# A transform chunk loaded one chunk later, and the two heads' maxima begun level

## The chip, the cores and the metric

The kernel runs on one core of a Trainium2 chip. The metric is device time in microseconds (us) of one execution; the time of the kernel before is the median of three timed executions, and its profile comes from one further execution. In the profile PE is the matrix engine's matmuls and PEld its weight loads, DVE the vector engine, ACT the scalar engine, POOL the GpSimd engine, and SP the queue from which nearly all transfers are issued.

## The reference

```python
def reference(A_x, A_dft_seq_re, A_dft_seq_im, A_dft_hid_re, A_dft_hid_im, B_x, B_wqkv, B_wo, gate_w):
    x = A_x                                    # 1 x 2048 x 512
    g = sigmoid((x * gate_w).sum(-1, keepdims=True))
    a = x @ A_dft_hid_re.T ; b = x @ A_dft_hid_im.T
    y = A_dft_seq_re @ a - A_dft_seq_im @ b    # 2048 x 2048 by 2048 x 512
    q, k, v = heads(x @ B_wqkv)                # 32 heads of 16
    p = softmax(q @ k.T * 16 ** -0.5)          # per head 2048 x 2048
    o = merge(p @ v) @ B_wo
    return g * y + (1 - g) * o
```

Everything is float32. The large products are made in three passes from a rounded part and a rest ("hi" and "lo"), which the kernel calls `h1, l1` or `ch, cl`.

## The kernel before

**Two streams beside each other.** The 32 heads are 16 pairs. Head 0 of a pair lies in the upper half of the partitions, head 1 in the lower half, from partition 64 on. A matmul on one half of the rows of PE runs beside one on the other half. So the kernel puts the transform (the DFT, matmuls with output `d` at L416) on one half and one head's attention on the other, and swaps the halves from segment to segment.

**The attention of a pair** has three kinds of work on PE. Maxima (`a_tile`, L222): a tile of raw scores, of which DVE takes the row maxima (L224). Scores (L722): the same product with the maxima folded in as two further rows, of which ACT makes exponentials (L723). Values (L758): the exponentials times v. The maxima of a head run `LEAD = 48` tiles ahead of its scores, out of 64 tiles for each head of a pair. The stacks `qs` and `ks` hold q and k of one pair; there are two of each, so pair p uses those of pair p-2. `load_stacks(p)` fills both with twelve transfers, six for head 0 first and then six for head 1 (L209, L210). It is put in line at unit 32(p-1)-1 of the plan, just ahead of the values of the last units of pair p-2, and its transfers wait until the last scores of that pair have read the stacks.

**The order is written out.** A segment is one half: a pattern of slots (`FULL`, for the 96 pairs of segments that carry the transform), each slot a transform matmul and beside it a score or a maximum of the other head, and at `|` the values. Even segments serve head 1, odd ones head 0. `FULL` has 16 slots with eight scores and eight maxima; the maxima are in slots 1, 4, 5, 8, 9, 11, 13 and 14, counted from 0.

**The start.** `four(range(4), *wre, ...)` makes the last rows ahead of the segments in four phases of twelve paired matmuls (L315). After matmuls 3 and 8 of a phase it calls `first_tiles`, which in the kernel before does something after matmul 3 only: a score of head 0 and a maximum of head 1, side by side.

**The transform's matrix** comes in 128 chunks of 256 KB (`w_seq`). `c_load` (L361) puts a chunk into one of two staging tiles (`craw`, in turn), `c_split` (L371 and L372, on POOL) makes `ch` and `cl` from it, which have three places in turn. Both are called from `dft_next` at the end of chunk i: `c_split(i + 3)` and then `c_load(i + 5)`, whose staging tile is the one that this split reads. A chunk is twelve transform matmuls on each half; of the sixteen that a pair of segments carries, its ends fall at slots 12, 8, and 4 and 16 of three pairs in turn. All transfers from SP are issued in program order and use eight completion semaphores in turn, so that a transfer also waits for the one eight places before it.

**POOL** also adds up the values' partial sums (L773), adds the two halves of the transform (L474) and makes the attention's output parts (`nh`, L85); several SP transfers (`yg`, `oh`, `o`) wait for these.

## Time and profile before

| | us |
|---|---|
| median of three timed executions (lowest, highest) | 1738.22 (1738.08, 1739.89) |
| the profiled execution's own time | 1735.85 |
| its span, first to last instruction | 1733.7 |
| PE busy (share of the span) | 1689.3 (97%) |
| DVE, ACT, POOL busy | 1373.9, 1249.5, 746.5 |
| granted clock of PE, mean | 0.99 |

PE is busy when at least one matmul is under way on it, on either half of its rows. The profile's views used below are the page's summary and chain of waits, the list of waits by engine, tables of busy time by stretch of time, and the timeline, in which rows of equal instructions that follow each other are merged (start, duration, count). In a timeline row the brackets give the idle time of the engine just before it and what ended it; where several semaphores are waited for, or where transfers share one, that name is only the likeliest.

### The profile page before, as it was taken

To read this page: it belongs to the slowest core of one execution; us is meant where nothing else is said; L and a number is where in the kernel's file an instruction comes from. 1 tells how busy PE (TensorE), PEld (TensorE's weight loads), DVE (VectorE), ACT (ScalarE), POOL (GpSimd) and SP (SyncE) were. 2 spreads that over 40 slices of the span, in tenths; PEclk is the share of its full clock that TensorE was granted. 3 is DMA by queue.
4 is the path that set the end of the run, shared out by engine and by line. 5 is a ranking of instruction groups with operands and counts; after the bars stand their busy time and mean duration, and the time that the engine had idled before them with its cause. 6 is when DMAs were issued, how large, how long until landed. Compare 5 with 4: busy or idle time off the path is not lost.

```text
span 1733.7 us, 34488 instructions
## 1 busy us (share of the span) xinstructions
PE 1689.3 (97%) x13072; PEld 1093.2 (63%) x13072; DVE 1373.9 (79%) x2283; ACT 1249.5 (72%) x2472; POOL 746.5 (43%) x807
## 2 busy tenths in 40 slices
PE   9999999999999999999999998999999899999998
PEld 7888766666656665665666665666666566655543
DVE  5448688888878887887888886888888787899954
ACT  5211388877778787777787786777778687787796
POOL 1115544544434555444444564445545456322230
PEclk9999999999999999999999999999999999999999
DMA  9963502113141425123164535133141525631014
GB/s 300 335 143 121 154 8 38 37 50 68 44 74 57 94 87 117 38 65 59 44 176 144 117 110 106 44 68 69 56 86 51 107 86 129 236 61 34 16 42 136
DMA packets 82486, 165.16 MB, mean 95 GB/s; under 512 B 19776, under 2 KB 20032, under 8 KB 78480
## 3 DMA queue, kind: packets, MB, share of 16 engines
q1 hardware_dynamic: 77968, 162.56, 36.1%
q8 instruction: 103, 1.69, 0.4%
q0 software_dynamic: 4352, 0.39, 0.3%
q14 instruction: 63, 0.52, 0.1%
HBM read 107.73 MB, written 54.52 MB: 94 GB/s over the span
## 4 chain that ended last, share of the span: by engine, by line
PE 89%; DMA 7%; SPq 1%; POOL 1%; ACT 1%; issue 1%; DVE 0%; DVEq 0%; POOLq 0%; ACTq 0%
PE d L416 34%; PE t L758 25%; PE t L222 10%; PE t L722 8%; PE t L315 4%; DMA ks<-qk 4%; DMA qs<-qk 2%; PE t L88 2%; PE t L89 2%; PE t L90 2%; PE t L333 1%; DMA craw<-w_seq 1%; PE t L739 1%; SPq L209 1%; SPq L210 1%
## 5 line engine op out<-in xcount | busy, mean ns | idle before, releaser
L224 DVE TENSOR_REDUCE mx<-t 128x1 f32<-128x512 f32 x2022 | 1255.1, 683 | 241.9 <-PE t L222 182.7
L723 ACT ACTIVATE pt<-t 128x512 f32<-128x512 f32 x2048 | 1038.1, 633 | 47.8 <-PE d L416 30.6
L722 PE MATMUL t<-qs,ks 50*128 50x512 f32 x2048 | 743.6, 414 | 0.9 <-ACT y L432 0.9
L222 PE MATMUL t<-ks,qs 48*128 48x512 f32 x2022 | 696.3, 403 | 32.0 <-DMA ks<-qk 17.7
L416 PE MATMUL d<-xab,ch 64*128 64x512 f32 x2016 | 649.3, 397 | 0.0
L758 PE MATMUL t<-pt,vt 128*32 128x512 f32 x3968 | 481.1, 602 | 0.0
L416 PEld LDWEIGHTS d<-xab,ch 64*128 64x128 f32 x2016 | 368.3, 185 | 132.7 <-issue 88.0
L222 PEld LDWEIGHTS t<-ks,qs 48*128 48x128 f32 x2022 | 368.3, 186 | 99.6 <-issue 29.9
L416 PE MATMUL d<-xab,cl 64*128 64x512 f32 x1008 | 400.3, 397 | 0.0
L722 PEld LDWEIGHTS t<-qs,ks 50*128 50x128 f32 x2048 | 368.8, 185 | 34.3 <-ACT pt L723 13.2
L773 POOL TENSOR_TENSOR osum<-osum,oe 128x512 f32<-128x512 f32 x217 | 279.6, 1288 | 169.5 <-ACT oe L767 154.2
L767 ACT COPY oe<-t 128x512 f32<-128x512 f32 x217 | 127.6, 588 | 242.8 <-PE t L758 241.7
L758 PEld LDWEIGHTS t<-pt,vt 128*32 128x32 f32 x3968 | 105.4, 109 | 232.7 <-issue 153.2
L371 POOL CAST ch<-craw 128x512 fp32r<-128x512 f32 x126 | 77.1, 612 | 373.0 <-PE t L722 341.8
L416 PEld LDWEIGHTS d<-xab,cl 64*128 64x128 f32 x1008 | 186.5, 185 | 67.6 <-issue 50.3
L372 POOL TENSOR_TENSOR cl<-craw,ch 128x512 fp32r<-128x512 f32 x126 | 162.1, 1287 | 10.2
L245 POOL DMA_DIRECT2D qs<-mt x128 | 72.0, 568 | 93.0 <-DVE mt L241 86.3
L416 PE MATMUL d<-wo_hl,o_hl 64*128 64x512 f32 (+1 forms) x270 | 72.5, 392 | 0.8 <-DVE yp_qs L597 0.8
L416 PE MATMUL d<-wre,xab 64*128 64x512 f32 x288 | 70.4, 389 | 0.0
L416 PEld LDWEIGHTS d<-wre,xab 64*128 64x128 f32 x288 | 52.9, 185 | 3.9
L416 PEld LDWEIGHTS d<-wo_hl,o_hl 64*128 64x128 f32 (+1 forms) x270 | 49.5, 185 | 4.8 <-DVE yp_qs L597 1.3
L88 PE MATMUL t<-xab,wh 128*128 128x512 f32 x128 | 50.2, 392 | 0.0
(121 smaller groups left out, 891.6 us busy)
## 6 DMA issues: line engine op xcount, KB each, us to landing
craw<-w_seq SPq DMA_DIRECT2D x128, 256.0 KB
qk<-hl SPq DMA_DIRECT2D x32, 512.0 KB
qs<-qk SPq DMA_DIRECT2D x96, 128.0 KB
ks<-qk SPq DMA_DIRECT2D x96, 128.0 KB
b<-hl SPq DMA_DIRECT2D x16, 512.0 KB
xab<-b SPq DMA_DIRECT2D x16, 512.0 KB
o<-osum SPq DMA_DIRECT2D x62, 128.0 KB
oh<-nh SPq DMA_DIRECT2D x12, 512.0 KB
```

Of the source, the lines that this page charges most:

```text
L88: nc.tensor.matmul(ps, sh, mh, start=first, stop=False)
L222: nc.tensor.matmul(ps, qs[p % 2][r, qt * P:(qt + 1) * P], ks[p % 2][r, kb * 512:(kb + 1) * 512], start=True, stop=True)
L224: user = nc.vector.tensor_reduce(mx[p % 2][:, h, qt, kb:kb + 1], ps, AX.X, ALU.max)
L245: (nc.sync, nc.gpsimd)[h].dma_start(rows.rearrange("v (q b c) -> v b q c", q=8, b=4)[:, b], mt[hf][32 * b + h:32 * b + 32:2])
L371: nc.gpsimd.tensor_copy(h1, raw)
L372: nc.gpsimd.tensor_tensor(l1, raw, h1.bitcast(F32), ALU.subtract)
L416: i = nc.tensor.matmul(self.ps, st[r], mv[r], start=not self.begun, stop=stop)
L722: nc.tensor.matmul(ps, ks[p % 2][rr, kt * P:(kt + 1) * P], qs[p % 2][rr, q0:q0 + 512], start=True, stop=True)
L723: return nc.scalar.activation(pts[u][:, 2 * qb + h], ps, AF.Exp, bias=0.0, scale=DH ** -0.5)
L758: nc.tensor.matmul(acc[32 * j:32 * j + 32], vt[:, kt, p, h:h + 32], pt[:, j], start=u == us[0], stop=u == us[-1])
L767: nc.scalar.copy(oe, acc)
L773: nc.gpsimd.tensor_tensor(o, o, oe, ALU.add)
```

## The change

There are two edits. First, `dft_next` calls `c_load(i + 4)` in place of `c_load(i + 5)`, and the extra first load, `c_load(4)`, goes. Chunk i+4 goes into the staging tile that was read by `c_split(i + 2)`, put in line one chunk end before; it is split at the next chunk end. Second, `first_tiles` issues a score of head 0 after matmul 3 and a maximum of head 0 after matmul 8, each alone in its slot, where it issued a score of head 0 and a maximum of head 1 together after matmul 3. After the four phases head 0 has four scores and four maxima done beyond the common lead, and head 1 none; before, head 0 had four more scores and head 1 four more maxima.

```diff
@@ real_next
             c_load(3)
             c_split(2)
-            c_load(4)
@@ dft_next
             c_split(i + 3)
-            c_load(i + 5)
+            c_load(i + 4)
@@ first_tiles
         if j == 3:
-            user = scores(*next(streams[0][0]), turn_of("a"))
-            a_tile(*next(streams[1][1]))
-            return user
+            return scores(*next(streams[0][0]), turn_of("a"))
+        a_tile(*next(streams[0][1]))
```

Lines after `first_tiles` and `real_next` move up by one or two: L722 becomes L721, L758 L757, L776 L775.

On PE, in the first of the four phases of the start (L315 are the phase's own matmuls, `x2` the two halves), before (-) and now (+):

```order
 L315 MATMUL t<-wre_1425,xab_175 128x512 x2
 L315 MATMUL t<-wre_1426,xab_175 128x512 x2
-L722 MATMUL t<-qs_934,ks_936 128x512
-L222 MATMUL t<-ks_936,qs_934 128x512
+L721 MATMUL t<-qs_934,ks_936 128x512
 L315 MATMUL t<-wre_1430,xab_175 128x512 x2
 L315 MATMUL t<-wre_1426,xab_175 128x512 x2
```

```order
 L315 MATMUL t<-wre_1431,xab_175 128x512 x2
 L315 MATMUL t<-wre_1427,xab_175 128x512 x2
+L222 MATMUL t<-ks_936,qs_934 128x512
 L315 MATMUL t<-wre_1428,xab_175 128x512 x2
 L315 MATMUL t<-wre_1432,xab_175 128x512 x2
```

The maximum no longer stands right behind the score, which ran on the other half of the rows; it comes five matmuls later and is of the same half.

On PE, where the first maximum of pair 3 stands (`ks_937` and `qs_935` are pair 3's stacks, `_936` and `_934` pair 2's; the brackets name the semaphores waited for, `DMAHW` those of SP's transfers). Before, an even segment, head 1:

```order
L722 MATMUL t<-qs_934,ks_936 128x512 [waits Activation_49]
L416 MATMUL d<-xab_178,ch 128x512
L222 MATMUL t<-ks_936,qs_934 128x512 [waits DVE_49]
L416 MATMUL d<-xab_178,cl 128x512
L222 MATMUL t<-ks_937,qs_935 128x512 [waits DMAHW5_49,DMAHW4_49,DMAHW6_49,DMAHW1_49,DMAHW7_49,DMAHW0_49,Activation_49]
L416 MATMUL d<-xab_178,ch 128x512
```

Now, the odd segment after it, head 0, and then the first maximum of head 1:

```order
L222 MATMUL t<-ks_936,qs_934 128x512 [waits DVE_49]
L416 MATMUL d<-xab_178,cl 128x512
L222 MATMUL t<-ks_937,qs_935 128x512 [waits DMAHW5_49,DMAHW2_49,DMAHW6_49,DMAHW1_49,DMAHW7_49,DMAHW0_49,Activation_49]
L416 MATMUL d<-xab_178,ch 128x512
...
L757 MATMUL t<-pt,vt 32x512 x7
L416 MATMUL d<-xab_175,ch 128x512 [waits Activation_49,Pool_49]
L721 MATMUL t<-qs_934,ks_936 128x512 [waits DVE_49]
L416 MATMUL d<-xab_175,ch 128x512
L222 MATMUL t<-ks_937,qs_935 128x512 [waits DMAHW5_49,DMAHW6_49,DMAHW4_49,DMAHW7_49,DMAHW3_49,DMAHW0_49]
```

The first use of a new pair's stacks moves by one whole segment, from slot 9 of an even one to slot 9 of the odd one after it; it is head 0's and waits for six transfers, and head 1's first, with six semaphores of its own, follows in slot 1 of the next segment.

On SP, where the transform begins (`craw` are the chunks' loads, `o` the values' sums). Before:

```order
L361 DMA craw<-w_seq 128x512 [waits DMAHW7_49,PE_49]
L361 DMA craw<-w_seq 128x512 [waits DMAHW0_49,PE_49]
L361 DMA craw<-w_seq 128x512 [waits DMAHW7_49,DMAHW1_49,Pool_49]
L776 DMA o_104<-osum 64x512 [waits DMAHW2_49,Pool_49]
L776 DMA o_104<-osum 64x512 [waits DMAHW3_49]
L361 DMA craw<-w_seq 128x512 [waits DMAHW4_49,DMAHW0_49,Pool_49]
```

Now:

```order
L361 DMA craw<-w_seq 128x512 [waits DMAHW7_49,PE_49]
L361 DMA craw<-w_seq 128x512 [waits DMAHW0_49,PE_49]
L775 DMA o_104<-osum 64x512 [waits DMAHW1_49,Pool_49]
L775 DMA o_104<-osum 64x512 [waits DMAHW2_49]
L361 DMA craw<-w_seq 128x512 [waits DMAHW7_49,DMAHW3_49]
L361 DMA craw<-w_seq 128x512 [waits DMAHW4_49,DMAHW0_49,Pool_49]
```

One load is gone from the head of the line, and every later place in it that loaded chunk i+5 loads chunk i+4. The number of the split that such a place waits for on POOL falls by one, so that it names a split of one chunk end earlier; the other transfers keep their order.

## The prediction

> **What bounds the kernel now.** I read the page first, for the engine that ends last.

> ```profile
> span 1733.7 us, 34488 instructions
> PE 1689.3 (97%) x13072; PEld 1093.2 (63%) x13072; DVE 1373.9 (79%) x2283; ACT 1249.5 (72%) x2472; POOL 746.5 (43%) x807
> PE 89%; DMA 7%; SPq 1%; POOL 1%; ACT 1%; issue 1%; DVE 0%; DVEq 0%; POOLq 0%; ACTq 0%
> ```

> PE is the bound, and the change takes no matmul from it. What can be had is PE's idle time, and the chain says of what kind that is: 7% of it are transfers. The list of PE's waits names them:

> ```profile
> PE t L222 <- DMA ks<-qk: 17.7, 3, 8.2
> PE t L222 <- DMA craw<-w_seq: 11.4, 4, 3.9
> PE t L222 <- DMA qs<-qk: 1.5, 1, 1.5
> ```

> Always it is a maximum (L222) that waits. I don't trust the name `craw` there, since no maximum reads a chunk; transfers share eight semaphores, and these waits lie at the same place as the others, a pair's first maximum. So PE stands still where the stacks of the next pair haven't landed.

> How much that costs I take from tables by stretch, the first two rows with the values' matmuls alone (16 to a segment), the third with all engines:

> ```profile
> 597.20:678.70 81.50, 26.94 (x224) 5.87 (x224) 1.00 0.30 92
> 345.10:1497.40 1152.30, 369.10 (x3040) 79.80 (x3040) 0.99 0.35 85
> 345.10:1497.40 1152.30, 1120.34 (x9121) 715.93 (x9120) 956.12 (x1574) 885.73 (x1754) 560.36 (x601) 0.99 0.35 85
> ```

> In an undisturbed stretch 224 / 16 = 14 segments take 81.5 us, 5.82 each. The transform's whole stretch has 3040 / 16 = 190 segments, which would take 1105.8 us at that pace and take 1152.3: **46.5 us too many**, over twelve loads of stacks. PE is idle for 1152.3 - 1120.3 = 32.0 of these. The other 14.5 are a slower PE, which shows behind the stalls (the column ahead of the last two is the granted clock):

> ```profile
> 1073.26 0.39 PE L416 MATMUL d<-xab,ch 64*128 64x512 f32 x1
> 1081.84 0.76 PE L222 MATMUL t<-ks,qs 48*128 48x512 f32 x1 [8.19 <-DMA ks<-qk]
> 1081.90:1085.60 3.70, 3.70 (x17) 2.41 (x21) 2.63 (x4) 1.59 (x3) 0.00 (x0) 0.50 0.24 88
> 790.82 0.47 PE L222 MATMUL t<-ks,qs 48*128 48x512 f32 x1 [2.88 <-DMA craw<-w_seq]
> 792.10:795.40 3.30, 3.30 (x17) 0.87 (x17) 1.71 (x3) 1.19 (x3) 0.00 (x0) 0.50 0.03 5
> 403.51 0.47 PE L222 MATMUL t<-ks,qs 48*128 48x512 f32 x1 [1.48 <-DMA qs<-qk]
> 403.50:405.00 1.50, 1.49 (x13) 1.39 (x13) 0.99 (x2) 0.76 (x2) 0.00 (x0) 1.00 0.02 8
> ```

> After 8.19 us idle, and after 2.88, PE gets half its clock for some microseconds; after 1.48 us, which is pair 3's stall, it keeps it. So a stall of 3 us costs nearly twice itself, and one below 1.5 only itself.

> [...]

> **Why the stacks are late.** The tenth pair's load is the worst. PE's row is the last score that reads the old stacks (slot 6 of its segment); the others are SP's line:

> ```profile
> 1055.13 0.39 PE L722 MATMUL t<-qs,ks 50*128 50x512 f32 x1
> 1046.63 10.35 SPq L361 DMA_DIRECT2D craw<-w_seq  x2
> 1060.27 0.33 SPq L475 DMA_DIRECT2D yg<-y  x1
> 1062.20 0.33 SPq L361 DMA_DIRECT2D craw<-w_seq  x1
> 1064.69 0.59 SPq L558 DMA_DIRECT2D oh<-nh  x1
> 1065.37 0.55 SPq L209 DMA_DIRECT2D qs<-qk  x1
> ...
> 1069.57 0.42 SPq L209 DMA_DIRECT2D qs<-qk  x1
> ...
> 1072.97 0.30 SPq L210 DMA_DIRECT2D ks<-qk  x1
> ...
> 1075.23 1.40 SPq L776 DMA_DIRECT2D o<-osum  x2
> ```

> The stacks are free at 1055.5, the first transfer leaves at 1065.4, 9.9 us later. From there the load needs 16.5 us until PE goes on at 1081.84; its last four pieces are held for the first four to land, 1.1 us apart ((1072.97 - 1069.57) / 3). The segment in question lasted 10 us too long. Pair 3 has the mild form:

> ```profile
> 383.51 0.39 PE L722 MATMUL t<-qs,ks 50*128 50x512 f32 x1
> 386.86 0.33 SPq L361 DMA_DIRECT2D craw<-w_seq  x1
> 387.28 0.38 SPq L209 DMA_DIRECT2D qs<-qk  x1
> ```

> Free at 383.9, left at 387.3: 3.4 us late, and a stall of 1.5. In both a chunk's load stands directly or nearly in front, waiting for the split of the chunk that has just ended, and the list of SP's waits has that as its largest entry:

> ```profile
> SPq L361 <- POOL cl L372: 489.8, 97, 13.0
> ```

> **The change part by part.**

> *The later first use.* The old first maximum of a pair was head 1's fifth of an even segment, the new one is head 0's fifth of the odd segment after it. That is one segment, 5.82 us more. Moreover head 0 needs only the six transfers that go first. In pair 10 they have landed by about 1075.2: the place in line at 1075.23 is eight behind the sixth, and waits for it. They are needed at 1073.65 (the old stall's start) + 5.82 = 1079.5, so 4.3 us are to spare even if the load starts no earlier. Head 1's first then stands in slot 1 of the next even segment: two segments less eight slots later than now, 11.64 - 8 x 0.23 = 9.8 us, so at 1083.4 against a landing by 1081.84: 1.6 us to spare. In pair 3, with a stall of 1.5, both spare more. I see none of the twelve that keeps a stall of its own.

> *The moved load.* At the place ahead of the stacks SP now waits for a split one chunk end earlier, which is long done. In pair 3 the next thing that holds it is the stacks themselves, so the load leaves up to 3.4 us earlier. In pair 10 `oh` still waits for POOL until 1064.69 and little is gained. This is a second cover on top of the first; I count nothing for it. The number of transfers falls by none (128 chunks, each still loaded once), only the line's first place goes.

> So the term is the whole 46.5 us, idle and half clock together, less what is left over: stalls below 1.5 us in one or two pairs, I put 0.5.

> *What the later chunk costs.* A chunk must now land between its place in line and the next chunk end. POOL's split shows the ends, and that until now it waited for PE and never for a transfer:

> ```profile
> L371 POOL CAST ch<-craw 128x512 fp32r<-128x512 f32 x126 | 77.1, 612 | 373.0 <-PE t L722 341.8 <-PE d L416 31.2
> 867.86 0.61 POOL L371 CAST ch<-craw 128x512 fp32r<-128x512 f32 x1 [5.55 <-PE t L722]
> 878.57 0.61 POOL L371 CAST ch<-craw 128x512 fp32r<-128x512 f32 x1 [4.64 <-PE d L416]
> 881.33 0.61 POOL L371 CAST ch<-craw 128x512 fp32r<-128x512 f32 x1 [0.78 <-PE d L416]
> 892.32 0.61 POOL L371 CAST ch<-craw 128x512 fp32r<-128x512 f32 x1 [6.79 <-PE t L722]
> qs<-mt POOLq DMA_DIRECT2D x128, 2.0 KB, 1.7
> ```

> The ends lie 10.7, 2.8 and 11.0 us apart; one in four is close, 32 in all. SP runs ahead, so a chunk usually leaves soon after the split before last, but where something stands in front it may leave at the end itself. How long 256 KB take to land no clean row tells. Below: 1.7 us, what 2 KB take. Above: 4.2 us, from the first piece of pair 10 (1065.37) to the ninth that waited for it (1069.57), plus 1.1 for the second 128 KB, 5.3 us. I take 4, near the upper row, as both are transfers from DRAM of the same order. Then POOL stands up to 1.2 us at a close end, 2.5 at worst. Behind a stack load, which holds the rings for 16.5 us, it may stand some 5. What is queued behind it on POOL: the sums (L773), for which ACT's next-but-one copy waits, and the stores on SP. But the chunk itself is used only three ends after the one where it is put in line, two after its split, over 13 us; and POOL has work for 560.36 of 1152.3 us. I cost it at nothing, with this cover; a hold beyond about 6 us, a segment, would reach ACT through the two buffers of sums.

> *The start.* Four maxima that ran beside a score now stand alone.

> ```profile
> 197.96 2.90 PE L315 MATMUL t<-wre,xab 64*128 64x512 f32 x24
> 200.70 0.39 PE L722 MATMUL t<-qs,ks 50*128 50x512 f32 x1
> 200.71 0.39 PE L222 MATMUL t<-ks,qs 48*128 48x512 f32 x1
> ```

> Twelve paired matmuls take 200.70 - 197.96 = 2.74 us, 0.23 a slot. At least four slots are added, 0.9 us; at most each maximum costs its full 0.39, 1.6 us. I take 1.0, nearest to the row of slots. The last of them frees the transform's bank some five slots later than before, with no room to spare, so nothing is gained here.

> *The sum.* 1735.85 (the profiled execution) - 46.5 + 0.5 + 1.0 = 1690.9 us. The median of the timed runs stands 2.4 us above the profiled one; I carry that over: **1693 us**.

> **The rivals.**

> *The stalls shrink but stay.* Head 0's margin is worked out with loads as they are now. If POOL, held by chunks, gives `oh` and `yg` later, three or four loads leave still later, and each stall of 3 us costs about 5 with its half clock. At most four such: +20, 1713; likelier two of 2 to 3 us, about 1700. For it: pair 10 has only 1.6 us for head 1. Against: the other loads spare more, and SP's largest wait goes.

> *It doesn't do what it says.* If the late start were the transfers' own pace and the added segment were eaten by chunks that now leave ahead of the stacks, each 256 KB (2.2 us at 1.1 per 128 KB), two of them would take 4.4 of the 5.82 us. Each load then gains 1.4 us, with the half clock that goes with it (46.5 / 32.0) 2.0, the twelve 25, and some 22 us stay: 1715. Against it: the chunks are moved, not added.

> *The chunk becomes the wait* (the other side). Mechanism: SP reaches a chunk only at the chunk end, POOL stands at each of the 32 close ends, and PE at the `ch` behind it. Price at the upper bound 2.5 us each, 80 us in all; at that price it would be 1693 + 80 = 1773, slower by 2%. It decides from the point where a chunk's split comes over 13 us late, or POOL holds the sums for more than a segment every time. For it: POOL is in order. Against: both covers are several times the price, and POOL is idle for half of the stretch.

> [...]

> **How the numbers follow.** All stalls gone, 1688 to 1697: 0.74. Stalls shrunk, 1697 to 1713: 0.16. It doesn't do what it says, 1703 to 1737: 0.05, with a fifth of that within 0.2%. The chunk becomes the wait: 0.05, of which 0.02 give back about all and 0.03 end slower. The lower end is the sum without left-overs and without the 2.4 us, should that be stall too: about 1689. Upwards the range goes into the second case until 2 in 10 are left out: 1688 to 1703. A measurement here can tell about 0.2%, 3.5 us, from no change. Faster by more: 0.94; within: 0.03; slower: 0.03.

> **What would show it.** The 190 segments of the stretch at 5.82 us each; no L222 with more than 1.5 us of idle time ahead of it; a granted clock of 1.00 through the stretch; SP's wait at L361 for `cl` far below 489.8 us; the first piece of pair 3's stacks right behind the last score. Wrong would be: a chunk's cast on POOL that waits for `craw` for over 6 us, copies on ACT that wait for POOL's sums, or PE's L416 waiting for `cl`. If the stalls are gone and the time isn't, the half clock or the close ends have taken it.

## The result, and the profile after

| | before | after |
|---|---|---|
| timed median, side by side (us) | 1739.06 | 1689.63 |
| lowest and highest | 1738.08, 1740.63 | 1689.11, 1690.03 |
| profiled execution (us) | 1735.85 | 1689.90 |

The changed kernel takes 0.9715 of the time of the one before (95% interval 0.9698 to 0.9732), 49.4 us less. It was measured twice more beside the experiments: 1690.09 us, 0.9735 (0.9713 to 0.9757), and 1690.52 us, 0.9733 (0.9717 to 0.975).

First the page of the changed kernel, its span, busy times and the chain that ended last:

```profile
span 1688.1 us, 34488 instructions
PE 1676.5 (99%) x13072; PEld 1089.9 (65%) x13072; DVE 1371.2 (81%) x2283; ACT 1246.1 (74%) x2472; POOL 747.3 (44%) x807
PE 98%; POOL 1%; issue 0%; DVE 0%; DMA 0%; ACT 0%; DVEq 0%; POOLq 0%; ACTq 0%
```

The 7% of transfers are gone from the chain. PE's busy time fell too, from 1689.3 to 1676.5 us with as many instructions (13072). These 12.8 us are mainly matmuls that ran at half the clock: by the trace's clock records PE was busy for 20.9 us at 0.50 in the transform's stretch before, and half of that is 10.5. PE's waits, the whole list (engine, line, what was waited for: us in total, times, longest):

```profile
PE t L159 <- DVE wch L156: 2.2, 1, 2.2
PE d L416 <- DVE yp_qs L596: 0.8, 1, 0.8
PE t L666 <- DVE on L660: 0.7, 1, 0.7
PE t L721 <- ACT y L432: 0.5, 1, 0.5
```

No maximum (L222) waits any more. The table by stretch, over the 190 segments of the transform, the values' matmuls alone and then all engines:

```profile
346.00:1452.00 1106.00, 365.55 (x3040) 79.34 (x3040) 1.00 0.37 88
346.00:1452.00 1106.00, 1106.00 (x9121) 711.23 (x9120) 952.93 (x1575) 882.74 (x1754) 560.90 (x601) 1.00 0.37 88
```

The same 3040 matmuls in 1106.0 us in place of 1152.3, PE busy for every one of them, at the full clock. Measured from the first values' matmul of a segment to that of the next, the stretch went from 1152.35 to 1105.87 us, 46.5 less, and each segment lasts 5.82 us, but for one that has 0.26 more in both kernels. Last, what SP waits for:

```profile
SPq L245 <- DVE mt L241: 329.9, 27, 25.4
SPq L775 <- POOL osum L772: 165.5, 17, 18.3
SPq L474 <- POOL y L473: 112.0, 14, 13.9
SPq L470 <- ACT y L469: 97.2, 15, 12.6
...
SPq L361 <- POOL cl L372: 47.3, 26, 5.7
```

The wait for a chunk's split fell from 489.8 to 47.3 us. But the first four grew, from 246.9, 95.6, 36.6 and 18.5: SP waits for what stands next in its line. How much of the gain hangs on this wait at all is what the experiments ask first.

### The profile page after: what moved, and what is told of

Same layout as the page of the kernel before. It is cut to its first block, busy times and chain, and to the rows that moved or that the text cites. A ratio compares the mean times of both kernels' runs of the same rounds, so it can differ in the third digit from the quotient of the medians.

```text
span 1688.1 us, 34488 instructions
## 1 busy us (share of the span) xinstructions
PE 1676.5 (99%) x13072; PEld 1089.9 (65%) x13072; DVE 1371.2 (81%) x2283; ACT 1246.1 (74%) x2472; POOL 747.3 (44%) x807
## 3 DMA queue, kind: packets, MB, share of 16 engines
q8 instruction: 103, 1.69, 0.4%
## 4 chain that ended last, share of the span: by engine, by line
PE 98%; POOL 1%; issue 0%; DVE 0%; DMA 0%; ACT 0%; DVEq 0%; POOLq 0%; ACTq 0%
PE d L416 40%; PE t L757 27%; PE t L222 10%; PE t L721 9%; PE t L315 4%; PE t L89 2%; PE t L88 2%; PE t L90 2%; PE t L333 1%; PE t L738 1%; PE t L416 0%; PE t L159 0%; POOL hl L292 0%; PE t L675 0%; DMA b<-hl 0%
## 5 line engine op out<-in xcount | busy, mean ns | idle before, releaser
L722 ACT ACTIVATE pt<-t 128x512 f32<-128x512 f32 x2048 | 1034.6, 631 | 9.5 <-PE t L721 9.3
L721 PE MATMUL t<-qs,ks 50*128 50x512 f32 x2048 | 740.2, 413 | 0.5 <-ACT y L432 0.5
L222 PE MATMUL t<-ks,qs 48*128 48x512 f32 x2022 | 689.8, 400 | 0.0
L416 PE MATMUL d<-xab,ch 64*128 64x512 f32 x2016 | 644.8, 394 | 0.0
L757 PE MATMUL t<-pt,vt 128*32 128x512 f32 x3968 | 477.5, 598 | 0.0
L416 PEld LDWEIGHTS d<-xab,ch 64*128 64x128 f32 x2016 | 366.7, 184 | 133.3 <-issue 92.2
L222 PEld LDWEIGHTS t<-ks,qs 48*128 48x128 f32 x2022 | 366.5, 186 | 62.4 <-DVE mx L224 27.4
L416 PE MATMUL d<-xab,cl 64*128 64x512 f32 x1008 | 397.9, 395 | 0.0
L721 PEld LDWEIGHTS t<-qs,ks 50*128 50x128 f32 x2048 | 366.9, 185 | 33.5 <-ACT pt L722 13.1
L757 PEld LDWEIGHTS t<-pt,vt 128*32 128x32 f32 x3968 | 105.0, 109 | 227.8 <-issue 148.8
L371 POOL CAST ch<-craw 128x512 fp32r<-128x512 f32 x126 | 77.4, 614 | 347.7 <-PE t L721 278.8
L416 PEld LDWEIGHTS d<-xab,cl 64*128 64x128 f32 x1008 | 185.6, 184 | 68.2 <-issue 51.1
L372 POOL TENSOR_TENSOR cl<-craw,ch 128x512 fp32r<-128x512 f32 x126 | 162.3, 1288 | 10.2
L416 PE MATMUL d<-wo_hl,o_hl 64*128 64x512 f32 (+1 forms) x270 | 72.6, 393 | 0.8 <-DVE yp_qs L596 0.8
L416 PE MATMUL d<-wre,xab 64*128 64x512 f32 x288 | 70.4, 389 | 0.0
L416 PEld LDWEIGHTS d<-wre,xab 64*128 64x128 f32 x288 | 52.9, 185 | 3.9 <-DVE mx L224 0.3
L416 PEld LDWEIGHTS d<-wo_hl,o_hl 64*128 64x128 f32 (+1 forms) x270 | 49.6, 185 | 4.6 <-DVE yp_qs L596 1.3
```

Source lines behind the costliest of these rows:

```text
L222: nc.tensor.matmul(ps, qs[p % 2][r, qt * P:(qt + 1) * P], ks[p % 2][r, kb * 512:(kb + 1) * 512], start=True, stop=True)
L371: nc.gpsimd.tensor_copy(h1, raw)
L372: nc.gpsimd.tensor_tensor(l1, raw, h1.bitcast(F32), ALU.subtract)
L416: i = nc.tensor.matmul(self.ps, st[r], mv[r], start=not self.begun, stop=stop)
L721: nc.tensor.matmul(ps, ks[p % 2][rr, kt * P:(kt + 1) * P], qs[p % 2][rr, q0:q0 + 512], start=True, stop=True)
L722: return nc.scalar.activation(pts[u][:, 2 * qb + h], ps, AF.Exp, bias=0.0, scale=DH ** -0.5)
```

## The experiments

Two theories stood at first. *The deadline* (D): the stalls go since the first use of a pair's stacks comes a segment later and needs only head 0's six transfers; the earlier place in SP's line does little. *The queue* (Q): the load of the stacks leaves earlier, since nothing ahead of it waits for a split, and that does it. Later runs ask what the margins are, and what the chunk's later load costs. Medians, and ratios to the kernel before on the same chip (its median there 1740.21 in the first group, 1736.84 in the second, 1735.67 in the third):

| run | us | ratio (95%) |
|---|---|---|
| e1_tiles | 1692.29 | 0.9732 (0.9713, 0.9751) |
| e2_load | 1726.49 | 0.9928 (0.9906, 0.9949) |
| e4_swap | 1694.10 | 0.9742 (0.9722, 0.9761) |
| e5_swap_before | 1692.98 | 0.9736 (0.9712, 0.9759) |
| a0_after, second group | 1690.09 | 0.9735 (0.9713, 0.9757) |
| e1_tiles_again | 1691.77 | 0.9746 (0.9724, 0.9768) |
| e3_level | 1690.87 | 0.9739 (0.9718, 0.9761) |
| e6_split_now | 1764.80 | 1.0165 (1.0141, 1.0189) |
| a1_after, third group | 1690.52 | 0.9733 (0.9717, 0.975) |
| e7_swap_load_oh | 1692.73 | 0.9747 (0.973, 0.9763) |
| e8_swap_load | 1692.10 | 0.9742 (0.9725, 0.9758) |

The changed kernel itself came out a little above what was expected of it both times (0.9735 for 0.970 to 0.973, 1690.52 for 1689.6 to 1690.4).

### One half of the change each

The second edit alone, on the kernel before:

```diff
         if j == 3:
-            user = scores(*next(streams[0][0]), turn_of("a"))
-            a_tile(*next(streams[1][1]))
-            return user
+            return scores(*next(streams[0][0]), turn_of("a"))
+        a_tile(*next(streams[0][1]))
```

> Only the second edit: the lone score and maximum of head 0 at the start; the chunks are loaded as before, c_load(i + 5). Theory D (the deadline: the first use one segment later, by the head whose six transfers go first, is what ends the stalls): all twelve stalls go although SP still waits for the splits, 190 segments at 5.82 us, 1690 us within 1.5. Theory Q (the queue: the stacks leave earlier since SP no longer waits for a split in front of them): stalls stay where the stacks leave over 6 us late, pair 10 and perhaps 5 and 6 to a smaller part, 1695 to 1710 us.

The first edit alone:

```diff
             c_split(2)
-            c_load(4)
...
             c_split(i + 3)
-            c_load(i + 5)
+            c_load(i + 4)
```

> Only the first edit: c_load(i + 4), the start with head 1's maxima as before. Theory Q: the stalls go, 1690 to 1695 us. Theory D: only the mild stalls go, those of pairs 3, 5, 8, 9, 11 and 12, whose stacks now leave within 0.2 us of the old ones' last score (6 to 7 us with their half clock), while 4, 6, 7, 10, 13 and 14, which leave 4 to 10 us late in the changed kernel as well, keep theirs: 1730 to 1734 us.

With the second edit alone no maximum waits, although SP waits for the splits as before; the row of SP's waits of e1_tiles:

```profile
SPq L361 <- POOL cl L372: 456.9, 96, 10.4
```

With the first edit alone that wait is gone (48.2 us) and the stalls are not; PE's waits of e2_load:

```profile
PE t L222 <- DMA ks<-qk: 15.4, 3, 8.2
PE t L222 <- DMA craw<-w_seq: 6.0, 2, 4.3
PE t L222 <- DMA qs<-qk: 2.3, 1, 2.3
```

So the deadline took the stalls: 1692.29 us by it alone (0.8 above what D allowed), 1726.49 by the queue alone. Q falls as the account of the whole, but its share was put too low: the first edit alone is worth 13.7 us (1740.21 - 1726.49; 9 to 16 by the ratio's interval) where 6 to 7 had been expected. It took the stalls of pairs 3, 5, 8, 9, 11 and 12, and those of 4, 6, 7, 10, 13 and 14 stayed, the longest at 8.2 us as before. Which pairs keep theirs is told by the time at which the first transfer of a pair leaves, counted from the end of the score that frees the stacks (slot 6 of its segment), in us:

| pair | 3 | 4 | 5 | 6 | 7 | 8 | 9 | 10 | 11 | 12 | 13 | 14 |
|---|---|---|---|---|---|---|---|---|---|---|---|---|
| before | 3.4 | 4.9 | 2.5 | 6.1 | 4.3 | 2.8 | 3.4 | 9.8 | 2.4 | 3.4 | 7.1 | 5.4 |
| after | 0.1 | 4.9 | 0.5 | 6.1 | 4.3 | 0.1 | 0.5 | 9.9 | 0.0 | 0.0 | 5.7 | 5.4 |

In six pairs something else in SP's line holds the load as long as the chunk did, or nearly; SP's row of the changed kernel for pair 10, where `oh` waits for POOL, shows it:

```profile
1041.56 0.33 SPq L474 DMA_DIRECT2D yg<-y  x1
1041.98 1.22 SPq L361 DMA_DIRECT2D craw<-w_seq  x1
1045.98 0.59 SPq L557 DMA_DIRECT2D oh<-nh  x1
1046.67 0.55 SPq L209 DMA_DIRECT2D qs<-qk  x1
...
1056.52 1.45 SPq L775 DMA_DIRECT2D o<-osum  x2
```

The pairs alone don't explain the whole 13.7 us. In the profiled executions, by the lengths of the segments, the six that went were worth 6.7 us, as expected, and the six that stayed cost some 4 us less than before; pair 7's stall, for one, is 2.31 us there and 2.88 before, and no half clock follows it (1.00 from 787.2 to 790.6). What is left is a difference between profiled and timed executions, and no run explains it.

On top of the second edit the first is worth little. A second run of that kernel beside the changed one:

> Only the second edit, timed closely. If the first edit is worth nothing once the first use is later, the same as the changed kernel within 0.5 us; if the 1.0 us that segment 196 lost in its first profile (ACT's cast of the attention's part, held by late transfers on SP) comes from SP's waits for the splits, 1 to 2 us slower.

> The changed kernel once more, for the comparison on one chip with the three below: 0.970 to 0.973 of the kernel before.

It took 1691.77 us (1691.65 to 1692.39) against 1690.09 (1689.65 to 1690.41): 1.7 us, in ranges that don't overlap. Most of it has one place, a segment that is 1.0 us longer in e1_tiles (1.3 in the second run). There ACT's `nh` waits for POOL's `no`, which waits for a load from SP; of e1_tiles:

```profile
1343.00 1.28 POOL L553 TENSOR_TENSOR no<-no 128x512 f32<-128x512 f32 x1 [8.87 <-DMA no<-r]
1344.31 0.62 ACT L84 CAST nh<-no 128x512 fp32r<-128x512 f32 x1 [1.80 <-POOL no L553]
```

In the changed kernel POOL's wait is 7.75 us and ACT's 0.69. On SP those loads (`no`) stand behind pair 13's stacks, which leave at 1323.54 in e1_tiles and at 1321.74 in the changed kernel; the last load of `no` leaves at 1338.76 and at 1336.55. So what the queue gives in the end is likely not the stacks but another load behind them in the line; no run changes that load alone.

### The margins, by the order of the twelve transfers

The changed kernel with head 1's six transfers first, so that head 0's first maximum needs the last of the twelve:

```diff
     def load_stacks(p):
-        for h in range(2):
+        for h in (1, 0):
```

> The changed kernel with the stacks loaded head 1 first: head 0's first maximum then needs the last six transfers. If the order of the twelve counts as the prediction has it (16.5 us from the first issue to the last landing), pair 10, whose load leaves at 1046.7 and whose first maximum stands at 1060.4, stalls for about 2.8 us and loses some 2 more to the half clock: 1693 to 1696 us. The others land in time (pair 13 with 1.5 us to spare). If one segment alone decides and the order does not matter: 1689.6 us, no stall.

The kernel before with that line alone; its first maximum is head 1's, which then needs only the first six:

> The kernel before with nothing changed but the order of the two heads' stacks, head 1's six transfers first, as head 1 makes the first use there. If six pieces (9.8 us) rather than twelve (16.5) are what the first use waits for, only pair 10 keeps a stall, about 1.5 us: 1689 to 1693 us, without the 1 us of the lone slots at the start. If the stalls come from the late leave of the load as such: 1725 to 1739 us.

Both came near what was expected: one pair stalls, the tenth, for 2.53 and 1.84 us (expected 2.8 and 1.5). For e4_swap that is in part luck: the half clock that was to add some 2 us did not come (the clock is 1.00 from 1063.9 to 1068.0), and the segment is 2.97 us longer than in the changed kernel. Its profiled execution (1693.78) stands 3.7 us above that of a0_after (1690.05); of the rest, 0.4 us is that its first phase began later, and 0.3 us is spread over the stretch. PE's rows, e4_swap's first, with the idle time in brackets:

```profile
1063.91 0.47 PE L222 MATMUL t<-ks,qs 48*128 48x512 f32 x1 [2.53 <-issue]
```

```profile
1055.74 0.46 PE L222 MATMUL t<-ks,qs 48*128 48x512 f32 x1 [1.84 <-DMA ks<-qk]
```

Two things follow. In e5_swap_before neither edit is made, the first use comes where it did, and SP waits for splits 460.8 us; still 1692.98 us result from one line. Six transfers in place of twelve ahead of the first use do nearly as much as the segment. And e4_swap shows when the last six have landed, by 1063.9, since nothing else of SP's line is changed; the account of the prediction below uses that.

### The four lone maxima

The changed kernel without them, so that both heads begin level at 48:

```diff
         if j == 3:
             return scores(*next(streams[0][0]), turn_of("a"))
-        a_tile(*next(streams[0][1]))
```

> The changed kernel without the four lone maxima: both heads begin with 48 maxima, head 0 with its four lone scores. The first uses come later still (head 1 in slot 1 two segments on), so no stall. The start is 0.9 us shorter if a lone maximum costs a slot of 0.23; the four maxima are made in the last odd segment, in places that stand empty in the changed kernel, for 0 to 0.9 us. So 0 to 0.9 us faster than the changed kernel.

A miss: 1690.87 us (1690.41 to 1691.04), 0.8 slower than the changed kernel beside it, where up to 0.9 faster was expected. The start is shorter nearly as expected: from the first matmul of the four phases to the first values it takes 17.31 us, not 18.06 as in a0_after. (Its first values come only 0.3 us earlier, at 211.70 and not 211.99, since its phases begin at 194.39 and not 193.93; that beginning lies between 193.5 and 194.4 in the runs' profiles, whatever the kernel.) But the last part of the attention took 181.25 us, not 180.38: four maxima that aren't made at the start are made there, in the last segments. A lone slot at the start was taken for lost; it is work done ahead. That makes the two kernels about equal; the rest of the 0.8 us stays open.

### What holds a chunk back

Each chunk loaded at the very chunk end at which its split is put in line:

```diff
             i = (c * NT + tt) * 4 + s // 4
+            if i:
+                c_load(i + 3)
             c_split(i + 3)
-            c_load(i + 4)
```

> The changed kernel with each chunk loaded still one chunk end later, just ahead of its own split: POOL then waits for the landing at nearly every end, 2 to 4 us each, some 300 us in all. If the cover (the chunk is used two ends after its split, over 13 us) hides it: PE stays at 5.82 us a segment and the time within 1 us of the changed kernel. If holding POOL reaches PE through the sums and ACT's copies or through the chunk: 5 to 80 us slower.

1764.80 us, 74.7 more than the changed kernel: the theory that even this stays hidden falls. POOL's, ACT's and PE's waits of e6_split_now:

```profile
POOL ch L371 <- DMA craw<-w_seq: 217.4, 39, 17.7
```

```profile
ACT oe L767 <- POOL osum L773: 60.5, 18, 8.8
```

```profile
PE t L722 <- ACT oe L767: 19.5, 15, 3.3
PE d L416 <- POOL ch L371: 9.0, 3, 6.3
```

The larger way is the one that the prediction named as a condition of its slower rival: POOL stands at a split, the sums behind it come late, ACT's copies wait for them, and PE for ACT. The smaller one, PE waiting for `ch`, is the rival's own. These two rows are 28.5 of the 74.7 us; behind its stalls PE also has half the clock for fifteen stretches of 3.4 us (its mean granted clock is 0.984, the changed kernel's 0.999). The row of POOL understates its waits, since some stand under a name of PE: counted from the chunk's end, or from when POOL is free if that is later, they are 336 us at 77 chunk ends (an estimate from the trace), where some 300 at nearly every end were expected. In the changed kernel the same two rows read:

```profile
POOL ch L371 <- DMA craw<-w_seq: 28.0, 8, 11.4
```

```profile
ACT oe L766 <- POOL osum L772: 1.3, 1, 1.3
```

Eight waits, and PE doesn't notice one. (The 11.4 us are POOL's idle time; only the part behind the chunk's end is the load's, as the account of the prediction shows.) The cover is there, and it is one chunk end deep: take that end away and it is gone.

### An attempt at something better

If six transfers suffice, the second edit's four lone slots can be saved: the start as before, the later chunk, head 1's transfers first, and for pair 10 the `oh` that holds its load put behind it in the plan (and so the like of two other pairs).

```diff
     def load_stacks(p):
-        for h in range(2):
+        for h in (1, 0):
...
-                    for step, du in enumerate((16, 20, 22)):
+                    for step, du in enumerate((16, 20, 24)):
```

> A version meant to beat both: the first edit (c_load(i + 4)), the start as before (score and head 1's maximum side by side, no lone slots), the stacks loaded head 1 first, and the last step of the attention's parts (cast, rest and the transfer oh) two units later, so that oh stands behind the stacks of pairs 6, 10 and 14 and no longer in front. Head 1's first maximum then needs six transfers, 9.8 us after a load that leaves 3 us earlier in pair 10: no stall. Against the changed kernel the start is 0.9 us shorter and nothing else differs: 0.5 to 1.0 us faster. If the lone slots cost nothing there: the same.

The same without the second line:

> The same without the later step, oh in front of those stacks. If oh is what holds pair 10's load, its stall stays: 1.5 to 2.5 us of idle time, with or without the half clock behind it, so 1.5 to 4 us slower than the version with the later step. If yg alone holds it: the same as that version.

> The changed kernel again, as the measure for the two below on their chip: 1689.6 to 1690.4 us.

e7_swap_load_oh has no stall at the stacks, and its first values come 1.2 us earlier (211.09 against 212.32; 0.75 of it is the shorter start, the rest that its phases began earlier), and still it takes 1692.73 us (1692.16 to 1693.36), 2.2 more than the changed kernel beside it. Three segments are 1.23, 0.27 and 1.75 us too long. POOL, ACT and PE in one of them:

```profile
1360.59 0.61 POOL L371 CAST ch<-craw 128x512 fp32r<-128x512 f32 x1 [3.74 <-DMA craw<-w_seq]
```

```profile
1363.84 0.58 ACT L766 COPY oe<-t 128x512 f32<-128x512 f32 x1 [3.09 <-POOL osum L772]
```

```profile
1364.48 0.50 PE L721 MATMUL t<-qs,ks 50*128 50x512 f32 x1 [0.69 <-ACT oe L766]
```

A split waits 3.74 us for its chunk, then come `cl` and two sums on POOL, and PE waits behind them: the chain of e6_split_now in small. e8_swap_load keeps the pair's stall, 1.67 us, and yet is no slower (1692.10, 1691.35 to 1692.64, where 1.5 to 4 us more than e7_swap_load_oh were expected): that `oh` holds the load is right, that moving it is free is not. No version that was run beats the changed kernel.

## Why the prediction was right, point by point

**The later first use: right, margins too.** All 46.5 us went. In pair 10 the prediction had 4.3 us to spare for head 0 and 1.6 for head 1. The two uses in the changed kernel are these rows of PE, the first in slot 9 of the segment that begins at 1058.14 (there e4_swap stalls, in a segment that begins at 1058.79), the second in slot 1 of the next:

```profile
1060.35 0.39 PE L222 MATMUL t<-ks,qs 48*128 48x512 f32 x1
...
1064.29 0.40 PE L222 MATMUL t<-ks,qs 48*128 48x512 f32 x1
```

The sixth transfer had landed by 1056.52, when the one eight places behind it left (SP's rows above): 3.8 us to spare. The twelfth is told by e4_swap, if the order of the heads changes nothing else: there PE goes on 5.12 us behind the start of its segment (1063.91 - 1058.79), which is 1063.3 here, so 1.0 us. The changed kernel's own trace has the last count of that transfer's semaphore at 1062.8, which would be 1.5.

**The moved load: right in kind, counted at nothing, worth 1.7 us by another way.** Pair 3's first piece now leaves right behind the last score (0.1 us, 3.3 us earlier than before), and pair 10's no earlier, both as told. As a second cover it gives nothing on top of the first. Most of the 1.7 us come by way of `no` and `nh`, which the prediction didn't look at.

**What the later chunk costs: right in the sum, somewhat short on the hold.** The prediction had POOL standing up to 2.5 us at a close end and some 5 behind a stack load, and had a hold beyond about 6 us reach ACT. POOL's longest idle time ahead of a chunk is 11.36 us, but the chunk's end, which this cast waits for as well, comes at 1060.2 only, so the load holds it for 5.6. The longest hold is another's: its chunk's end is at 1422.9, the load leaves behind a stack load at 1425.86, and POOL, free from 1425.58 on, stands for 7.8 us. The row names PE, but in a0_after the same place names `craw` (7.60 us). ACT then loses 1.29 us to the sum behind it, as was said, and PE nothing. (Another hold, of 6.4 us with the chunk's end at 585.0, costs not even ACT anything. Chunk ends are counted on PE by L416's matmuls, 24 to a chunk.) POOL's rows, then ACT's:

```profile
1065.82 0.61 POOL L371 CAST ch<-craw 128x512 fp32r<-128x512 f32 x1 [11.36 <-DMA craw<-w_seq]
1433.36 0.61 POOL L371 CAST ch<-craw 128x512 fp32r<-128x512 f32 x1 [7.78 <-PE t L222]
1436.61 0.59 ACT L766 COPY oe<-t 128x512 f32<-128x512 f32 x1 [1.29 <-POOL osum L772]
```

So the length of a hold alone doesn't tell its price: 3.74 us at another end, in e7_swap_load_oh, reached PE. The rival "the chunk becomes the wait" had its mechanism right in part: with one chunk end less, in e6_split_now, it cost 74.7 us, more by the sums than by `ch`. The prediction had put 80 on it, by 2.5 us at each of the 32 close ends; that the two are near is luck.

**The start: right in kind, a little high.** The first values came 0.98 us later (212.13 for 211.15) against 1.0. Of that 0.22 us is only that this execution's phases began later (194.06 for 193.84). The four phases themselves last 13.07 us in place of 12.06, so the four lone maxima cost 0.25 each; 0.26 comes back before the first values, and the start's own cost is 0.75.

**The sum: its carried-over term was mis-sized.** Terms from the two profiled executions, in us:

| term | predicted | measured |
|---|---|---|
| transform's stretch | -46.5 + 0.5 left over | -46.5 |
| start | +1.0 | +1.0 (0.75 its own) |
| rest of the attention, end, time outside the span | 0 | -0.5 |
| timed median less profiled execution | +2.4 | -0.3 |

With 1735.85 they give 1690.9 and 1689.9 for the profiled execution. The step that failed is "I carry that over": the 2.4 us by which the timed runs stood above the profiled one belonged to the kernel before, not to the measurement. The runs fit with stalls as their source: within one chip the kernel before spread from 1728.63 to 1742.98, the changed one, which has none, from 1689.65 to 1690.41. That each execution falls differently onto the clock's windows (last section) would explain it, but is only argued: no run takes that apart. The prediction had named the case, as the reason for its lower end.

**The half clock: the price was about right, the boundary wrong.** That a stall of 3 us costs nearly twice itself came near in the kernel before: behind its stalls of 2.88 and 3.11 us the segment and the one after it lasted 4.87 and 5.12 us more than two of 5.82, 1.7 and 1.6 times the stall. That the length alone decides, with a boundary between the 1.48 us that kept the clock and the 2.88 that lost it, did not hold: e5_swap_before's 1.84 us cost the clock (0.50 from 1057.3 to 1060.7), and e4_swap's 2.53 us did not (1.00 from 1063.9 to 1068.0). Nothing was left over, so it moved no number.

## What to carry to other kernels

Where an in-order line of transfers is late, look first at when and how much of a load is needed: a first use one segment later, or six transfers in place of twelve ahead of it, took stalls of which a shorter wait in the line took only half, since in the other pairs the next transfer in it waited as long. Before a load is put later, count the chunk ends between its landing and its use, and what else stands in line on the engine that waits for it: here one end later was free in the changed kernel, and two cost 75 us. And a stalled kernel's gap between timed and profiled runs is not a constant to be carried over to one without stalls.

## What the runs showed of the hardware

```profile
501.90:505.30 3.40, 3.40 (x19) 0.51 0.00 0
693.10:696.50 3.40, 3.40 (x17) 0.50 0.00 1
696.50:699.90 3.40, 3.40 (x32) 1.00 0.02 5
```

The two windows at the half clock hold 19 and 17 matmuls, the one at the full clock 32. Two stalls of e2_load show that the length of a stall alone does not decide. First PE's rows, then the windows behind them:

```profile
497.27 0.47 PE L222 MATMUL t<-ks,qs 48*128 48x512 f32 x1 [1.72 <-DMA craw<-w_seq]
787.25 0.47 PE L222 MATMUL t<-ks,qs 48*128 48x512 f32 x1 [2.31 <-DMA qs<-qk]
```

```profile
499.10:502.50 3.40, 3.40 (x17) 0.56 (x16) 1.16 (x2) 0.64 (x2) 0.00 (x0) 0.50 0.00 0
787.20:790.60 3.40, 3.35 (x29) 1.80 (x29) 2.48 (x4) 1.72 (x3) 0.00 (x0) 1.00 0.04 16
```

Behind the stall of 1.72 us the clock was 0.50, behind that of 2.31 it stayed at 1.00. Laid on the grid that starts at 499.1, the first has 1.59 us in one window; the second falls into two, 0.87 and 1.44. The 2.53 us of e4_swap fall into two windows as well, 1.32 and 1.21, and kept the clock; the 1.84 us of e5_swap_before lie in one and lost it. Worked out so for the windows of every run, each with the grid of its own half clock (an estimate, since the ends of matmuls in the trace are modelled), the clock was lost behind every full-clock window of the records with more than 1.7 us idle and behind none with 1.2 or less. In the kernel before it was lost behind 1.73 us (the window from 1071.97 on) and kept behind 1.51 (from 1269.94 on). Between 1.2 and 1.7 us the idle time alone does not decide, as two such windows of e6_split_now show, each with the one behind it:

```profile
1386.81:1390.22 3.41, 2.18 (x17) 1.00 0.19 68
1390.22:1393.63 3.41, 1.03 (x4) 0.50 0.00 0
1485.80:1489.21 3.41, 1.72 (x16) 1.00 0.98 113
1489.21:1492.62 3.41, 0.00 (x0) 1.00 0.55 151
```

Behind 1.23 us idle (3.41 - 2.18) the clock was lost, and behind 1.69 it was kept. What else counts stays open.
